# A gated product that reads its gate in PSUM, four output buffers, an undivided last row and a new order list

## The chip, the cores and the metric

The kernel runs on one core of one Trainium2 chip. The metric is the device time of one execution in microseconds; before the change the median of three runs was 163.64 us (162.80, 163.64, 165.22). A core has five engines that run side by side and wait for each other by semaphores: TensorE (PE, matrix products, results in PSUM), VectorE (DVE), ScalarE (ACT), GpSimd (POOL) and SyncE (SP, here only an issuer of DMAs).

## The reference

Sliding-window attention with sink tokens, and behind it a gated feed-forward block over the same sequence. Four batches, 8 heads of 64, 768 positions, window 128, 4 sinks; in the second half 512 model columns and 2 x 512 hidden columns.

```
scores = q @ k.T / 8, kept where key < 4 or 0 <= query - key < 128
x      = softmax(scores) @ v            # heads side by side: 4 x 768 x 512
h      = gelu(x @ w_in)                 # 1024 columns
u, v   = h[..., :512], h[..., 512:]
v_n    = (v - mean) / sqrt(var + 1e-6) * g_ln
v_s    = w_sg @ v_n + b_sg              # along the 768 positions
out    = x + (u * v_s) @ w_out
```

## The kernel before

The attention works on pairs of heads: 16 pairs n, four to a batch. For a pair, k and q are loaded, cast to bf16 on POOL or DVE (cast_k, cast_q), turned on PE and copied out of PSUM (turn, cols), or turned by a DMA for the last pairs. The scores come in three groups per pair (sc), an exponential on ACT leaves PSUM (exp), a mask is put on by DVE or POOL (band), the values are summed on PE (pv), and DVE divides (rcp, x). x is turned to columns xT by PE or by a DMA.

The block works on a batch b. hv makes the v half, 128 positions at a time, hu the u half, 128 hidden columns f by 384 positions (half m). ACT puts the gelu on (gelu_v, gelu_u), DVE takes mean and variance (bn), vn is the normalised v. The spatial product is eight tiles per batch: for f and m, six matmuls in two parts (sp..a, sp..b) fill half a bank of PSUM (tile vs); gate multiplies by g and adds the bias b_bc on DVE; gT multiplies by u into the tile gT, bf16 in SBUF. Then six projections pj of 128 positions each read gT, o adds x on DVE into an output buffer o_sb and a store issued on SP sends it out.

No engine chooses its order at run time. FIRST lists all operations by name, and `Planner.run` emits them in that order, so each engine's program is the sublist that falls on it. TAKERS says which engine takes an operation that several could do. A name has the batch or pair first: gate201 is batch 2, f = 0, m = 1; pj23 is batch 2, row 3. `Room` counts buffers: PSUM has six banks for these tiles, two in room s (scores, and in the last batch also vs and o_ps) and four in room m (everything else); o_sb has three buffers, gv two. In the last batch the output may also use the buffers of k_f and q_f.

Lines that the prediction speaks of: L858 the spatial matmul, L870 gate, L878 gT, L902 the projection, L913 o, L922 the store, L248 casts and copies on DVE or POOL, L632 and L630 the masks on DVE, L305 and L310 the masks on POOL, L670 the values, L689 x.

Of the kernel before, what the change touches and what calls it, by code (L numbers as in the profile page):

```python
# [49 lines left out]
class Planner:  # L50
# [40 lines left out]
    "load_k0 iden blank warm night dark nil zero_b0 zero_a0 zero_a2 zero_a3 load_q0 raw_a low_a "  # L91
# [86 lines left out]
def kernel(  # L178
# [65 lines left out]
    def copy(e, dst, src):  # L244
        if e == "ACT":
            nc.scalar.copy(dst, src)
        else:
            eng[e].tensor_copy(dst, src)  # L248


    NV = 6
    WARM = 8
    AHEAD = (0, 1)
    HALVES = 4
    LONG = ()
    BY_DMA = (11,12,13,14,15)
# [1068 lines left out]
```

## Time and profile before

| | us |
|---|---|
| median of three runs | 163.64 |
| the profiled execution | 162.83 |
| its span, first to last instruction | 161.1 |
| PE busy | 152.0 |
| DVE busy | 129.4 |
| ACT busy | 106.1 |
| POOL busy | 84.4 |
| first hv matmul of batches 0, 1, 2, 3 | 26.2, 66.75, 98.26, 129.69 |
| last matmul group ends | 155.85 |

The span is what the trace shows of the execution; the 1.7 us around it belong to the time too. In the rows that follow, a group of instructions is named by its line, engine and operation, with output and inputs; x8 is a count. A row of a stretch (from:to) gives its length, the busy time of each engine in it with the number of instructions, the granted clock, and the share of the DMA engines. A row of the timeline begins with start and duration in us.

### The profile page before, as it was taken

What the parts mean: (1) busy time and instruction counts of PE and PEld (TensorE: products, weight loads), DVE (VectorE), ACT (ScalarE), POOL (GpSimd) and SP (SyncE); (2) the same over time, 40 slices, a digit from 0 to 9 for tenths busy, and PEclk for the clock granted to TensorE, in tenths of its full rate; (3) what the DMA queues carried; (4) which work ended last, traced back from release to release, by engine and by line L of the source; (5) the groups of instructions that cost most, each with busy time, mean ns of one, the idle gap of its engine ahead of it and who ended that gap; (6) DMA issues with size and microseconds to landing.
All of it is one profiled execution on the core that took longest, in us unless ns stands there. A gap on an engine that the chain in (4) does not pass through costs nothing.

```text
span 161.1 us, 4019 instructions
## 1 busy us (share of the span) xinstructions
PE 152.0 (94%) x1562; PEld 88.1 (55%) x1562; DVE 129.4 (80%) x283; ACT 106.1 (66%) x142; POOL 84.4 (52%) x127
## 2 busy tenths in 40 slices
PE   6899999999999799999999999999999999999960
PEld 2346565576656656456656654455575645565530
DVE  3768486889799998497999889779998779768870
ACT  6368887789977687878967776684887158910100
POOL 3342891067859958777956745189568402300000
PEclk9999999999999999999999999999999999999998
DMA  4969999999999789899798799999922942030182
GB/s 152 352 171 312 204 179 191 226 348 336 327 233 307 222 103 260 210 347 284 180 215 195 192 186 276 194 259 214 215 81 78 162 157 78 2 135 1 69 319 78
DMA packets 67878, 32.43 MB, mean 201 GB/s; under 512 B 56564, under 2 KB 64772, under 8 KB 67856
## 3 DMA queue, kind: packets, MB, share of 16 engines
q1 hardware_dynamic: 65472, 29.39, 71.5%
q0 software_dynamic: 2384, 2.75, 10.7%
q8 instruction: 13, 0.21, 0.6%
q14 instruction: 9, 0.07, 0.1%
HBM read 24.81 MB, written 6.29 MB: 193 GB/s over the span
## 4 chain that ended last, share of the span: by engine, by line
PE 65%; DVE 19%; DMA 8%; issue 3%; ACT 1%; POOL 1%; SPq 0%; DVEq 0%; POOLq 0%
PE vs L858 14%; PE o_ps L902 10%; PE hv L745 10%; PE hu L787 10%; PE sc L604 7%; DMA out_dram<-o_sb 5%; PE av L670 5%; PE sc L584 4%; PE cps L544 3%; DVE o_sb L913 3%; DVE x L689 3%; DMA q_f<-in_q_dram 2%; DVE gv L870 2%; DVE st L767 2%; DVE ex L632 2%
## 5 line engine op out<-in xcount | busy, mean ns | idle before, releaser
L621 ACT ACTIVATE ex<-sc 128x1024 bf16<-128x1024 f32 x48 | 47.4, 1025 | 14.2 <-PE sc L604 14.2
L858 PE MATMUL vs<-wsgT,vn 128*128 128x384 bf16 x192 | 35.4, 327 | 0.1
L795 ACT ACTIVATE uT<-hu 128x384 bf16<-128x384 f32 x32 | 15.3, 490 | 14.3 <-PE hu L787 14.0
L858 PEld LDWEIGHTS <-vn 128*128 128x128 bf16 x192 | 17.6, 98 | 12.6 <-issue 1.3
L902 PE MATMUL o_ps<-w_out_sb,gT 128*128 128x512 bf16 (+1 forms) x100 | 23.7, 371 | 0.1
L787 PE MATMUL hu<-xT,w_in_sb 128*128 128x384 bf16 x128 | 23.1, 326 | 0.0
L305 POOL TENSOR_SCALAR_AFFINE_SELECT ex<-ex 128x512 bf16<-128x512 bf16 (+1 forms) x24 | 15.9, 663 | 13.5 <-ACT ex L621 13.3
L745 PE MATMUL hv<-w_in_sb,xT 128*128 128x512 bf16 x96 | 22.2, 379 | 0.3 <-DMA xT<-x 0.2
L870 DVE SCALAR_TENSOR_TENSOR gv<-vs,g_sb,b_bc 128x384 bf16<-128x384 f32 x32 | 19.3, 611 | 2.3 <-PE vs L858 1.7
L913 DVE TENSOR_TENSOR o_sb<-o_ps,x 128x512 f32<-128x512 f32 (+1 forms) x25 | 16.3, 663 | 4.5 <-PE o_ps L902 2.3
L767 DVE BATCH_NORM_STATS2 st<-v_all 128x6 f32<-128x512 f32 x24 | 16.2, 674 | 4.1 <-ACT v_all L756 4.0
L604 PE MATMUL sc<-qT,kT 64*128 64x256 bf16 (+2 forms) x320 | 19.0, 251 | 0.0
L670 PEld LDWEIGHTS <-ex 128*128 128x128 bf16 x480 | 16.2, 97 | 4.2 <-issue 2.1
L670 PE MATMUL av<-v_sb,ex 128*128 128x65 bf16 x352 | 17.3, 193 | 1.0 <-DVE o_sb L913 1.0
L689 DVE TENSOR_TENSOR x<-av,rcps 128x384 bf16<-128x384 f32 x32 | 17.3, 554 | 0.8
L878 DVE TENSOR_TENSOR gT<-gv,uT 128x384 bf16<-128x384 bf16 x32 | 15.8, 507 | 1.5 <-ACT uT L795 0.5
L787 PEld LDWEIGHTS <-w_in_sb 128*128 128x128 bf16 x128 | 12.3, 98 | 8.1
L756 ACT ACTIVATE v_all<-hv 128x512 f32<-128x512 f32 x24 | 13.5, 598 | 4.5 <-PE hv L745 4.2
L248 POOL CAST cast<-k_f 128x768 bf16<-128x768 f32 x14 | 12.5, 891 | 7.5 <-DMA k_f<-in_k_dram 7.4
L745 PEld LDWEIGHTS <-xT 128*128 128x128 bf16 x96 | 9.1, 98 | 11.5 <-DMA xT<-x 0.7
L248 POOL CAST v_sb<-v_f 128x768 bf16<-128x768 f32 x16 | 13.5, 860 | 3.1 <-DMA v_f<-in_v_dram 3.0
L248 POOL CAST cast<-q_f 128x768 bf16<-128x768 f32 x14 | 12.6, 898 | 4.6 <-DVE cast L248 2.3
(69 smaller groups left out, 198.8 us busy)
## 6 DMA issues: line engine op xcount, KB each, us to landing
k_f<-in_k_dram SPq DMA_DIRECT2D x16, 384.0 KB, 5.2
q_f<-in_q_dram SPq DMA_DIRECT2D x16, 384.0 KB, 5.2
v_f<-in_v_dram SPq DMA_DIRECT2D x16, 384.0 KB, 6.5
out_dram<-o_sb SPq DMA_DIRECT2D x23, 256.0 KB, 3.8
wsg<-in_moe_w_sg_dram POOLq DMA_DIRECT2D x2, 576.0 KB, 10.4
w_in_sb<-in_moe_w_in_dram POOLq DMA_DIRECT2D x2, 512.0 KB, 6.8
w_out_sb<-in_moe_w_out_dram POOLq DMA_DIRECT2D x1, 512.0 KB, 8.4
b_bc<-in_moe_b_sg_dram SPq DMA_DIRECT2D x1, 384.0 KB
```

Of the source, the lines that this page charges most:

```text
L248: eng[e].tensor_copy(dst, src)
L604: nc.tensor.matmul(sc.tile[row:row + keys, h, col:col + m], kT.tile[rows, k0:k0 + keys], qT.tile[rows, q0:q0 + m], start=not by_pe, stop=n ...
L621: nc.scalar.activation(out=ex.tile, in_=sc.tile, func=AF.Exp, scale=scale)
L670: nc.tensor.matmul(av.tile[:, m, h, :], ex.tile[:, h, col:col + 128], val, start=first, stop=(m == HT - 1 and h == 1 and at == len(steps) ...
L689: nc.vector.tensor_mul(x.tile[:, hp, HT * c:HT * (c + 1), :].rearrange("p i (h d) -> p i h d", h=2), av.tile[:, :, :, 0:64], rcp.to_broadc ...
L745: nc.tensor.matmul(ps.tile[:, 0:512], xT.tile[:, c, 128 * j:128 * (j + 1)], w_in_sb[:, c, DF:], start=(c == 0), stop=(c == KD - 1))
L767: nc.vector.bn_stats(out=st.tile, in_=v_all.tile[:, j, :])
L787: nc.tensor.matmul(ps.tile[:, 0:NH], w_in_sb[:, c, 128 * f:128 * (f + 1)], xT.tile[:, c, NH * m:NH * (m + 1)], start=(c == 0), stop=(c == ...
L858: nc.tensor.matmul(ps.tile[:, 0:NH], vn.tile[:, si, 128 * f:128 * (f + 1)], wsgT[:, si, cols], start=(si == 0), stop=(si == NT - 1))
L870: nc.vector.scalar_tensor_tensor(out=gv.tile, in0=ps.tile[:, 0:NH], scalar=g_sb[:, f:f + 1], in1=b_bc[:, cols], op0=ALU.mult, op1=ALU.add)
L902: nc.tensor.matmul(ps.tile[:, 0:w], gT.tile[:, c, 128 * t:128 * (t + 1)], w_out_sb[:, c, cols], start=(c == 0), stop=(c == KU - 1))
L913: nc.vector.tensor_add(o_sb.tile[:, 0:w].rearrange("p (h d) -> p h d", d=128), ps.tile[:, 0:w].rearrange("p (h d) -> p h d", d=128), x.til ...
```

## The change

Gate no longer writes a bf16 tile gv in SBUF: it writes its result back over the f32 tile vs in PSUM, and gT reads it there. So the bank is held until gT is done. The room gv goes down to one buffer, which only the general path uses, and o_sb has four buffers in place of three. The projection of the last batch's row 4 is no longer made in two column halves (HALVES). The planning costs of gT and of the stores are changed in the program's text, and FIRST and TAKERS are new as a whole; of them one line stands here.

```diff
-    "store11 gT211 pj21 cols_x15 store22 hv30 o21 store21 hv34 gT201 gelu_v30 hv32 gelu_v32 "
+    "xT12 store14 xT13 xT14 pj22 o22 store03 sp221a turn_x15 cols_x15 gate201 sp221b gate221 "
...
-        s=2, m=4, k_f=4, q_f=4, v_f=4, cast=4, cast_v=2, kT=5, qT=4, ex=8, x=2, xT=2,
-        v_all=1, mv=2, uT=2, vn=2, gT=2, gv=2, o_sb=3, st=4).items()}
+        v_all=1, mv=2, uT=2, vn=2, gT=2, gv=1, o_sb=4, st=4).items()}
...
-    HALVES = 4
+    HALVES = None
...
-        ps, gv = Buf([R[r] for r in rooms]), Buf(R["gv"])
+        ps = Buf([R[r] for r in rooms])
...
         def gate(_):
-            gv.tile = tile_of("gv")
             nc.vector.scalar_tensor_tensor(
-                out=gv.tile, in0=ps.tile[:, 0:NH], scalar=g_sb[:, f:f + 1], in1=b_bc[:, cols],
-                op0=ALU.mult, op1=ALU.add)
+                out=ps.tile[:, 0:NH], in0=ps.tile[:, 0:NH], scalar=g_sb[:, f:f + 1],
+                in1=b_bc[:, cols], op0=ALU.mult, op1=ALU.add)
...
-            nc.vector.tensor_mul(gT.tile[:, f, cols], gv.tile, uT.tile[:, f, cols])
+            nc.vector.tensor_mul(gT.tile[:, f, cols], ps.tile[:, 0:NH], uT.tile[:, f, cols])
...
-            f"gT{b}{f}{m}", {"DVE": 500 if b < B - 1 else 365}, mul,
+            f"gT{b}{f}{m}", {"DVE": 560}, mul,
...
-            use=[gv, uT, gT], rank=rank - 1)
+            use=[ps, uT, gT], rank=rank - 2000)
```

In TAKERS, the casts of k0, q0, q1 and k3 go from DVE to POOL and that of q2 the other way; the masks band72 and band81 go from POOL to DVE and band41 the other way; of the 24 vn, DVE has 16 in place of 17; the copy of k4 goes from ACT to DVE and that of k5 from DVE to ACT.

Three places show how the programs of the engines move. The first is DVE in the spatial stage of batch 0, from its first gate on; before, with gv as the gate's output:

```order
L870 SCALAR_TENSOR_TENSOR gv<-vs,g_sb,b_bc 128x384
L248 COPY kT<-cps 128x768
L870 SCALAR_TENSOR_TENSOR gv<-vs,g_sb,b_bc 128x384
L878 TENSOR_TENSOR gT<-gv,uT 128x384 x2
L632 TENSOR_TENSOR ex<-ex,mask_71 128x1024
L870 SCALAR_TENSOR_TENSOR gv<-vs,g_sb,b_bc 128x384
L630 TENSOR_TENSOR ex<-ex,mask 128x2x384
L870 SCALAR_TENSOR_TENSOR gv<-vs,g_sb,b_bc 128x384
L878 TENSOR_TENSOR gT<-gv,uT 128x384
```

And DVE at the same place now:

```order
L869 SCALAR_TENSOR_TENSOR vs<-vs,g_sb,b_bc 128x384
L877 TENSOR_TENSOR gT<-vs,uT 128x384
L869 SCALAR_TENSOR_TENSOR vs<-vs,g_sb,b_bc 128x384
L877 TENSOR_TENSOR gT<-vs,uT 128x384
L632 TENSOR_TENSOR ex<-ex,mask_71 128x1024
L869 SCALAR_TENSOR_TENSOR vs<-vs,g_sb,b_bc 128x384 x2
L877 TENSOR_TENSOR gT<-vs,uT 128x384 x2
L869 SCALAR_TENSOR_TENSOR vs<-vs,g_sb,b_bc 128x384
```

Each gT now follows its gate at once or behind one more gate; the copy of kT and the mask of 384 columns are gone from between them.

The second place is POOL at the head of the program, from the two masks of the constant tile on, where the first casts of k and q stand; before:

```order
L305 AFFINE_SELECT ex<-ex 128x2x128
L310 AFFINE_SELECT ex<-ex 128x2x128
L390 MEMSET vsink 4x8
L248 CAST vsink<-raw 4x8x64
L248 CAST cast<-k_f 128x2x6x64 x2
L248 CAST cast<-q_f 128x2x6x64
L248 CAST v_sb_74<-v_f 128x12x64
L248 CAST cast<-q_f 128x2x6x64
L248 CAST v_sb_75<-v_f 128x12x64
L427 DMA w_in_sb<-in_moe_w_in_dram 128x4x512
```

POOL at the same place now:

```order
L305 AFFINE_SELECT ex<-ex 128x2x128
L310 AFFINE_SELECT ex<-ex 128x2x128
L248 CAST cast<-k_f 128x2x6x64
L248 CAST cast<-q_f 128x2x6x64
L248 CAST cast<-k_f 128x2x6x64
L248 CAST cast<-q_f 128x2x6x64
L248 CAST cast<-k_f 128x2x6x64
L248 CAST v_sb_74<-v_f 128x12x64
L248 CAST cast<-k_f 128x2x6x64
L248 CAST cast<-q_f 128x2x6x64
```

The sink rows (vsink) have gone to DVE, and the first two pairs are cast on POOL; the load of w_in is issued next behind these rows, ahead of the second cast of v.

The third place is DVE at the end of its program, from the last spatial tiles to the last output; before:

```order
L870 SCALAR_TENSOR_TENSOR gv<-vs,g_sb,b_bc 128x384
L878 TENSOR_TENSOR gT<-gv,uT 128x384
L913 TENSOR_TENSOR o_sb<-o_ps,x 128x512 x3
L913 TENSOR_TENSOR o_sb<-o_ps,x 128x256
L913 TENSOR_TENSOR o_sb<-o_ps,x 128x512
L913 TENSOR_TENSOR o_sb<-o_ps,x 128x256
L913 TENSOR_TENSOR o_sb<-o_ps,x 128x512
```

DVE at the same place now:

```order
L912 TENSOR_TENSOR o_sb<-o_ps,x 128x512
L869 SCALAR_TENSOR_TENSOR vs<-vs,g_sb,b_bc 128x384
L877 TENSOR_TENSOR gT<-vs,uT 128x384 x2
L912 TENSOR_TENSOR o_sb<-o_ps,x 128x512 x6
```

Behind the last gT stand six outputs of full width in place of five and two halves. On PE both programs end with pj23, and on SP with store23.

More of the change, by code (lines that the diff above doesn't have):

```diff
@@ L90 @@
 FIRST = (
[L91 removed]
[64 rows of a table removed]
+    "load_k0 iden load_q0 raw_a night blank nil zero_a3 zero_a1 zero_b3 warm zero_a0 dark mask "
[64 rows of a table added]
 )
 TAKERS = (
[L158 to L161 removed]
@@ L162 @@
-    "cols_k2:DVE cast_q2:POOL cols_q2:DVE cols_x2:ACT cast_k3:DVE cols_k3:ACT cast_q3:POOL "
-    "cols_q3:DVE cols_x3:DVE vn00:DVE vn01:DVE vn02:DVE vn03:DVE vn04:DVE vn05:ACT cols_k4:ACT "
-    "cols_q4:ACT band41:DVE band42:POOL cols_k5:DVE cols_q5:ACT band51:POOL band52:POOL "
+    "zero_a0:ACT zero_a1:DVE zero_a2:DVE zero_a3:DVE low_a:DVE zero_b0:DVE zero_b1:DVE "
+    "zero_b2:ACT zero_b3:DVE low_b:POOL cols_g:DVE cols_w0:DVE cols_w1:ACT cols_w2:ACT "
+    "cols_w3:DVE cols_w4:DVE cols_w5:DVE cast_k0:POOL cols_k0:DVE cast_q0:POOL cols_q0:ACT "
@@ L165 @@
+    "cols_x0:ACT cast_k1:POOL cols_k1:DVE cast_q1:POOL cols_q1:DVE cols_x1:ACT cast_k2:POOL "
+    "cols_k2:DVE cast_q2:DVE cols_q2:DVE cols_x2:DVE cast_k3:POOL cols_k3:ACT cast_q3:POOL "
+    "cols_q3:DVE cols_x3:DVE vn00:DVE vn01:DVE vn02:ACT vn03:ACT vn04:DVE vn05:DVE cols_k4:DVE "
+    "cols_q4:ACT band41:POOL band42:POOL cols_k5:ACT cols_q5:ACT band51:POOL band52:POOL "
     "cols_k6:ACT cols_q6:ACT band61:POOL band62:POOL cols_k7:ACT cols_q7:ACT band71:POOL "
-    "band72:POOL cols_x7:DVE cols_k8:ACT cols_q8:ACT band81:POOL band82:POOL vn10:DVE vn11:DVE "
@@ L170 @@
+    "band121:POOL band122:POOL vn20:DVE vn21:DVE vn22:ACT vn23:ACT vn24:ACT vn25:DVE "
     "band131:POOL band132:POOL band141:POOL band142:POOL band151:POOL band152:POOL cols_x15:ACT "
-    "vn30:DVE vn31:DVE vn32:ACT vn33:ACT vn34:DVE vn35:ACT"
+    "vn30:DVE vn31:ACT vn32:ACT vn33:ACT vn34:DVE vn35:DVE"
 )
```

14 lines of the change are left out of this document (5 added, 9 removed), and 126 rows, old and new, of the table FIRST.

## The prediction

> **What bounds the kernel now.** I read the page first: busy time of each engine, then the chain that ended last.
>
> ```profile
> span 161.1 us, 4019 instructions
> PE 152.0 (94%) x1562; PEld 88.1 (55%) x1562; DVE 129.4 (80%) x283; ACT 106.1 (66%) x142; POOL 84.4 (52%) x127
> PE 65%; DVE 19%; DMA 8%; issue 3%; ACT 1%; POOL 1%; SPq 0%; DVEq 0%; POOLq 0%
> ```
>
> TensorE is busy 94% of the span and holds 65% of the chain; VectorE comes second with 80% and 19%. An average hides the stages, so next I cut the span at the first hv matmul of each batch, with one more cut where the spatial matmuls of batch 0 begin.
>
> ```profile
> core 0: us, PE busy (x) PEld busy (x) DVE busy (x) ACT busy (x) POOL busy (x), PEclk, DMA share, GB/s
> 26.00:40.46 14.46, 14.46 (x126) 8.86 (x126) 11.26 (x25) 12.47 (x22) 6.01 (x10) 1.00 1.12 286
> 40.46:66.75 26.29, 25.28 (x337) 16.02 (x337) 23.32 (x44) 20.34 (x24) 21.46 (x29) 1.00 1.00 246
> 66.75:98.26 31.51, 31.13 (x341) 17.98 (x340) 27.83 (x58) 25.39 (x34) 22.05 (x33) 1.00 0.97 221
> 98.26:129.69 31.43, 31.29 (x315) 17.98 (x315) 27.45 (x60) 19.82 (x28) 19.06 (x30) 1.00 0.90 185
> 129.69:155.85 26.16, 26.12 (x146) 14.05 (x144) 21.25 (x49) 10.41 (x18) 2.51 (x4) 1.00 0.25 94
> ```
>
> From 26.00 to 155.85 us PE is idle for 129.85 - 128.29 = 1.6 us (the sums of these rows), and the clock is full throughout. So little can be won in the middle: only the stretch from 40.46 has a PE gap of 1.01 us. In the third and fourth stretch DVE is busy 88% and 87% beside a full PE, with 3.7 and 4.0 us of room. The chain through the second stretch says who holds PE there, and the waits put a size on it.
>
> ```profile
> 53.53 1.00 DVE gT L878 x2
> 54.53 0.57 issue
> 55.11 0.69 DVE o_sb L913
> 55.79 0.04 issue
> 55.84 0.71 PE av L670 x18
> ...
> PE av L670 <- DVE o_sb L913: 1.0, 1, 1.0
> DVE o_sb L913 <- DMA out_dram<-o_sb: 2.1, 2, 1.4
> ```
>
> There gT and o run on DVE while PE waits for the bank that o frees: the 1.0 us. DVE itself waits 2.1 us in two places for an output buffer that a store still reads.
>
> **The multiplication gT.** It goes from two bf16 tiles in SBUF to one f32 operand in PSUM and one in SBUF. The rows of the same engine show both kinds (ns: least, median, most).
>
> ```profile
> L878 DVE TENSOR_TENSOR gT<-gv,uT x32: 344/359/1305, 43.6 to 151.4; 128x384 bf16<-128x384 bf16 x32
> L870 DVE SCALAR_TENSOR_TENSOR gv<-vs,g_sb,b_bc x32: 601/611/618, 41.6 to 150.3; 128x384 bf16<-128x384 f32 x32
> L689 DVE TENSOR_TENSOR x<-av,rcps x32: 518/557/559, 20.1 to 126.6; 128x384 bf16<-128x384 f32 x32
> L913 DVE TENSOR_TENSOR o_sb<-o_ps,x x25: 414/683/692, 55.1 to 155.9; 128x512 f32<-128x512 f32 x23, 128x256 f32<-128x256 f32 x2
> ```
>
> The nearest row to the new gT is x: 128x384, one operand in PSUM, 557 ns. I take 557, against a median of 359 now. But today's gT spreads up to 1305 ns, and the three kinds with one operand in PSUM hardly spread at all (601 to 618). What stretches it stands beside it on POOL:
>
> ```profile
> 53.26 0.82 POOL L248 CAST v_sb<-v_f 128x768 bf16<-128x768 f32 x1
> 54.02 0.95 POOL L248 CAST cast<-k_f 128x768 bf16<-128x768 f32 x1
> ...
> 53.45 1.74 DVE L878 TENSOR_TENSOR gT<-gv,uT 128x384 bf16<-128x384 bf16 x2
> ```
>
> Two gT take 1.74 us while POOL casts without a pause. So the price must be taken batch by batch (gT alone):
>
> ```profile
> core 0: us, DVE busy (x), PEclk, DMA share, GB/s
> 41.00:56.00 15.00, 5.79 (x8) 1.00 1.04 275
> 80.00:101.00 21.00, 3.62 (x8) 1.00 0.99 213
> 111.00:135.00 24.00, 3.66 (x8) 1.00 0.65 146
> 135.00:154.00 19.00, 2.78 (x8) 1.00 0.16 59
> ```
>
> Afterwards each batch has 8 x 0.557 = 4.46 us of gT: **-1.3 us in batch 0, +0.8 in batches 1 and 2 each, +1.7 in batch 3**, together +2.0 us of DVE.
>
> The Trainium skill, "VectorE: DVE Perf Modes", section "The perf-mode tier table", speaks against the change: a tensor_tensor of bf16 in SBUF runs at two results a cycle, with any PSUM operand at one. By that alone every gT would cost 557 - 344 = 0.21 us more, 6.8 us over 32; the trace agrees on the bare durations (344 against 557) and not on the sum, since the batches above already pay for the stretching.
>
> **The sum, stage by stage.**
>
> - Batch 0 (40.46 to 66.75). gT gives 1.3 us back; the kT copy of pair 4 (a DVE COPY of 0.95 us here) now stands ahead of the first gate; one more full mask product (row below) is on DVE. That is -1.33 - 0.95 + 0.73 = -1.55 us of DVE. PE idled 1.01 us. What is late next is ACT, whose exponentials feed the values, busy 20.34 of 26.29. I take **-0.7 us**, ends -1.5 and 0.
>
> ```profile
> L632 DVE TENSOR_TENSOR ex<-ex,mask x12: 675/730/1304, 45.1 to 122.1; 128x1024 bf16<-128x1024 bf16 x12
> 42.12 0.95 DVE L248 COPY kT<-cps 128x768 bf16<-128x768 bf16 x1
> ```
>
> - Batches 1 and 2. +1.6 us of DVE beside a PE with 0.5 us of gaps. DVE's room in those stretches (3.7 and 4.0 us) covers it on average, but gates come in bunches and PE waits for the banks they free; half of it shows: **+0.8**, ends 0 and 1.6.
> - Batch 3. +1.7 on DVE, 21.25 + 1.7 = 22.95 us against 26.16 of PE: hidden, **0**. The last gT ran from 151.43 and its first reader comes after two projections that don't need it (5.35 / 6 = 0.89 us each), so 0.2 us more is covered too.
>
> ```profile
> 149.81 0.81 PE L787 MATMUL hu<-xT,w_in_sb 128*128 128x384 bf16 x4
> 150.46 5.35 PE L902 MATMUL o_ps<-w_out_sb,gT 128*128 128x512 bf16 x28
> ...
> 151.43 0.36 DVE L878 TENSOR_TENSOR gT<-gv,uT 128x384 bf16<-128x384 bf16 x1 [0.47 <-ACT uT L795]
> 155.85 0.69 DVE L913 TENSOR_TENSOR o_sb<-o_ps,x 128x512 f32<-128x512 f32 x1 [0.20 <-PE o_ps L902]
> ```
>
> - The bank. Until now gate freed it; now gT does, 0.6 us later, and where gT has to wait for u, later still. Queued behind a waiting gT are the other gates, rcp and x of the attention, and PE waits for their banks. Batches 0 to 2 share four banks, so 24 x 0.6 / 4 = 3.6 us is the upper end; lower end 0, since the new order issues gT right behind its gate. Near the lower end, because PE has almost no gaps on banks now: **+0.5**.
> - The gate's write. No row shows DVE writing PSUM. Its f32 output is wider; o, with f32 output, takes 683 ns for 512 elements and x, with bf16, 557 for 384, which is 0.98 ns for each of 128 more elements: width costs nothing. I take 0. Ends: 0.07 us each way (gate against o, 683 - 611), 2.3 us over 32, both ways since a write to another memory may end sooner or later.
> - Output buffers. The 2.1 us of waits may go; one was in front of the statistics of batch 1, but store03 now stands behind o22, so o03 keeps its buffer through batches 1 and 2 and three are left to turn. **-0.3**, ends -2.1 and 0.
> - The head. The casts of k0 and q0 go from DVE to POOL. q0 is on the chain:
>
> ```profile
> 5.40 0.82 DVE cast L248
> ...
> L248 POOL CAST cast<-q_f 128x768 bf16<-128x768 f32 x14 | 12.6, 898 | 4.6 <-DVE cast L248 2.3
> 18.19 0.98 POOL L427 DMA_DIRECT2D w_in_sb<-in_moe_w_in_dram  x1
> ```
>
> 898 - 820 is +0.08, and POOL does four casts in a row where DVE took part: **+0.2**, upper end one cast, 0.9. POOL also issues the w_in load (18.19); it is behind one cast of v fewer and three casts of k and q more, of which POOL waited 2.3 us for one, so it moves little.
> - The last row undivided: one o of 0.68 for two of 0.42, PE's 28 matmuls in the tail become 24 of the same columns, and both programs end with pj23, o23 and its store: 0.
> - The rest of the new order (stores, loads, casts, hu and sp exchanged within their batch) leaves the work of each engine as it was; on SP's queue stores 10, 11, 14 and 00 come earlier, 03, 05, 15 and 20 later, each an issue on a queue with nothing busy behind it but loads. I price it at 0, ends -1 and +1.
>
> Sum: -0.7 + 0.8 + 0 + 0.5 + 0 - 0.3 + 0.2 = **+0.5 us** on the profiled execution of 162.83 us, so 163.3. The median of the three runs is 163.64, 0.8 above that execution; on the median's scale I say **164.1 us**.
>
> **Rivals.**
>
> 1. *The stretching goes and carries more with it: 162.4.* If gT no longer meets POOL, POOL's own casts get shorter too (1.28 us for the one at 48.73, against 0.82 at 53.26), so batch 0 gains its whole 1.5 us, DVE's waits for buffers go with 1.0, and batches 1 and 2 stay hidden under PE: 163.64 - 1.5 - 1.0 + 0.8 + 0.5 = 162.4. For it: the spread of gT and its absence with one PSUM operand. Against: PE has only 1.6 us of gaps. The Trainium skill has this as a rule ("SBUF — State Buffer", section "Who interferes with whom"): two SBUF inputs on DVE contend with a reading POOL, one does not; the trace agrees as far as the rows go (601 to 618 against 344 to 1305).
>
> ```profile
> 48.73 1.28 POOL L248 CAST cast<-k_f 128x768 bf16<-128x768 f32 x1
> ```
>
> 2. *Banks become the bound: 167.2, slower.* In the spatial stages of batches 0 to 2 PE finds all four banks held by results waiting for gT. It decides once the extra hold, 0.6 us for each of 24, is no longer covered by banks that stand empty; in full it is 3.6 us: 163.64 + 3.6 = 167.2. Against it: in the order, hardly a gate has more than one operation before its gT.
> 3. *Writing PSUM is dear: 166.1.* +0.07 us on each gate as well; 2.3 us on a DVE that has 3.7 us of room in a stretch, of which most shows in batches 0 to 2: 164.1 + 2.0.
> 4. *The buffers do not turn:* o03 parks one and nothing is gained there, while the rest holds: 164.4, inside the forecast's own case.
>
> **How the numbers follow.** The forecast with rival 4 has 0.54, rival 1 0.23, rival 2 0.12, rival 3 0.11. Two per cent of 163.64 is 3.3 us, about what a measurement of this kernel can tell from no change: faster below 160.4, slower above 166.9. Rival 1 passes the lower bound only with both unknown costs at their good ends (0.05 in all); rival 2 passes the upper one, and rival 3 in part: 0.13. Within: 0.82. The range reaches from 161.8, a little past rival 1, to 166.6, past rival 3; rival 2 stays outside.
>
> **What would show it.** gT with a median near 557 ns and a most below 600; the gate at 611; eight gT of batch 0 in 4.5 us; the PE gap near 55 us gone or shorter; gate and gT back to back on DVE. I am wrong if PE rows L858 or L670 wait for DVE gT for more than 1 us in sum, if the gate is over 0.68, or if hv of batch 1 starts over 1 us later than 66.75.

## The result, and the profile after

The changed kernel takes 162.5 us, the median of 20 runs (161.09 to 166.14), beside 163.72 us for the kernel before in 20 runs on the same chip (162.73 to 165.27). The ratio is **0.9912, with a 95% interval of 0.9883 to 0.9941**: a little faster, where the forecast was a little slower. The time lies in the predicted range and within 2% of the time before, but +0.5 us was forecast and -1.2 us came. (Ratios, here and below, leave out executions that took over 1.5% longer than the fastest of the same kernel, medians keep them, so the two do not agree in every row; the profiled executions of b_zero and a_gv2 are of that kind.)

The profiled execution took 161.09 us, with a span of 159.2 us against 161.1. First the page of the changed kernel: its span, the busy times of the engines, and the shares of the chain that ended last.

```profile
span 159.2 us, 4002 instructions
PE 150.8 (95%) x1558; PEld 87.1 (55%) x1558; DVE 130.0 (82%) x281; ACT 107.5 (68%) x143; POOL 83.5 (52%) x126
PE 76%; DVE 7%; DMA 7%; POOL 3%; ACT 2%; SPq 1%; issue 1%; POOLq 0%; ACTq 0%
```

DVE has gone from 19% of the chain to 7%, and PE from 65% to 76%. The busy times hardly moved. Next the view by stretches of the changed kernel, cut at the first hv matmul of each batch and at the end of the last projection. The table behind it has the kernel before cut at the same places (its first hv matmuls start at 26.08, 66.75, 98.26 and 129.53).

```profile
core 0: us, PE busy (x) PEld busy (x) DVE busy (x) ACT busy (x) POOL busy (x), PEclk, DMA share, GB/s
24.58:65.06 40.48, 39.75 (x461) 24.99 (x459) 34.65 (x73) 33.41 (x45) 26.84 (x38) 1.00 1.01 249
65.06:96.40 31.34, 30.64 (x342) 18.10 (x341) 28.03 (x58) 25.37 (x34) 20.88 (x30) 1.00 0.96 215
96.40:127.24 30.84, 30.84 (x311) 17.27 (x310) 27.26 (x59) 20.72 (x29) 19.67 (x31) 1.00 0.94 210
127.24:154.40 27.16, 27.14 (x147) 14.15 (x145) 22.88 (x47) 10.62 (x18) 2.51 (x4) 1.00 0.24 90
```

| stretch | before | after | difference |
|---|---|---|---|
| start to the first hv matmul of batch 0 | 26.08 | 24.58 | -1.50 |
| to the first hv of batch 1 | 40.67 | 40.48 | -0.19 |
| to the first hv of batch 2 | 31.51 | 31.34 | -0.17 |
| to the first hv of batch 3 | 31.27 | 30.84 | -0.43 |
| to the end of the last projection | 26.28 | 27.16 | +0.88 |
| to the end | 5.3 | 4.8 | -0.5 |

The four stretches from the first hv to the end of the last projection, which hold all of gate and gT, come to 129.7 us before and 129.8 after. The +0.88 of batch 3 is one thing: pj20 stood ahead of hv30 and stands behind hv35 now, and a projection is 0.89 us of PE. With it left out, batch 2 is 0.45 us longer and not 0.43 shorter. What is left is the head, -1.50, and the tail, -0.5. The tail is the same work in another execution: two repeats of the changed kernel (after2 and after3, below) had 5.3 and 5.0 there.

Now the groups of the two operations that the change rewrites (ns: least, median, most), and gT alone in the spatial stage of each batch.

```profile
L877 DVE TENSOR_TENSOR gT<-vs,uT x32: 542/557/558, 41.7 to 149.8; 128x384 bf16<-128x384 f32 x32
...
L869 DVE SCALAR_TENSOR_TENSOR vs<-vs,g_sb,b_bc x32: 609/616/626, 41.0 to 148.6; 128x384 f32<-128x384 f32 x32
```

```profile
core 0: us, DVE busy (x), PEclk, DMA share, GB/s
38.00:56.00 18.00, 4.34 (x8) 1.00 1.20 300
78.00:101.00 23.00, 4.36 (x8) 1.00 0.97 197
108.00:135.00 27.00, 4.44 (x8) 1.00 0.61 152
135.00:154.00 19.00, 4.31 (x8) 1.00 0.25 97
```

gT now costs 557 ns wherever it stands, and the spread up to 1305 ns is gone. The gate costs 616 ns for 611. These are the predicted sizes, almost to the digit, and they are not where the time went.

### The profile page after: what moved, and what is told of

The parts are those of the page before. It is cut to its first block, busy times and chain, and to the rows that moved or that the text cites. A ratio compares the mean times of both kernels' runs of the same rounds, so it can differ in the third digit from the quotient of the medians.

```text
span 159.2 us, 4002 instructions
## 1 busy us (share of the span) xinstructions
PE 150.8 (95%) x1558; PEld 87.1 (55%) x1558; DVE 130.0 (82%) x281; ACT 107.5 (68%) x143; POOL 83.5 (52%) x126
## 3 DMA queue, kind: packets, MB, share of 16 engines
HBM read 24.81 MB, written 6.29 MB: 195 GB/s over the span
## 4 chain that ended last, share of the span: by engine, by line
PE 76%; DVE 7%; DMA 7%; POOL 3%; ACT 2%; SPq 1%; issue 1%; POOLq 0%; ACTq 0%
PE vs L858 20%; PE o_ps L901 12%; PE hv L745 10%; PE sc L604 9%; PE av L670 8%; PE hu L787 7%; PE cps L544 4%; PE sc L584 3%; DMA k_f<-in_k_dram 3%; DMA q_f<-in_q_dram 2%; DVE vn L834 2%; PE xps L720 2%; POOL cast L248 2%; DMA xT<-x 1%; DVE o_sb L912 1%; DVE mv L820 1%
## 5 line engine op out<-in xcount | busy, mean ns | idle before, releaser
L901 PE MATMUL o_ps<-w_out_sb,gT 128*128 128x512 bf16 x96 | 23.0, 379 | 0.0
L869 DVE SCALAR_TENSOR_TENSOR vs<-vs,g_sb,b_bc 128x384 f32<-128x384 f32 x32 | 19.5, 619 | 2.6 <-PE vs L858 1.3
L305 POOL TENSOR_SCALAR_AFFINE_SELECT ex<-ex 128x512 bf16<-128x512 bf16 (+1 forms) x23 | 15.4, 670 | 9.4 <-ACT ex L621 9.1
L248 POOL CAST cast<-k_f 128x768 bf16<-128x768 f32 x16 | 13.4, 836 | 12.1 <-DMA k_f<-in_k_dram 12.0
L670 PEld LDWEIGHTS <-ex 128*128 128x128 bf16 x480 | 16.7, 97 | 4.1 <-issue 1.4
L877 DVE TENSOR_TENSOR gT<-vs,uT 128x384 bf16<-128x384 f32 x32 | 17.4, 554 | 0.9
L670 PE MATMUL av<-v_sb,ex 128*128 128x65 bf16 x352 | 18.0, 194 | 0.1
L912 DVE TENSOR_TENSOR o_sb<-o_ps,x 128x512 f32<-128x512 f32 x24 | 16.2, 684 | 1.5 <-PE o_ps L901 1.4
```

Of the source, the lines that this page charges most:

```text
L670: nc.tensor.matmul(av.tile[:, m, h, :], ex.tile[:, h, col:col + 128], val, start=first, stop=(m == HT - 1 and h == 1 and at == len(steps) ...
L869: nc.vector.scalar_tensor_tensor(out=ps.tile[:, 0:NH], in0=ps.tile[:, 0:NH], scalar=g_sb[:, f:f + 1], in1=b_bc[:, cols], op0=ALU.mult, op1 ...
L877: nc.vector.tensor_mul(gT.tile[:, f, cols], ps.tile[:, 0:NH], uT.tile[:, f, cols])
L901: nc.tensor.matmul(ps.tile[:, 0:w], gT.tile[:, c, 128 * t:128 * (t + 1)], w_out_sb[:, c, cols], start=(c == 0), stop=(c == KU - 1))
L912: nc.vector.tensor_add(o_sb.tile[:, 0:w].rearrange("p (h d) -> p h d", d=128), ps.tile[:, 0:w].rearrange("p (h d) -> p h d", d=128), x.til ...
```

## The experiments

In this table the first-hv column is of the profiled execution, and "from there" is the time from the first hv to the end of the last projection (before: 26.08 and 129.7; after: 24.58 and 129.8). Each kernel ran beside the kernel before on the same chip; the runs are spread over several chips. All compute the whole result.

| kernel | ratio to before | 95% interval | first hv | from there |
|---|---|---|---|---|
| b_gate: before, gate in PSUM | 1.0635 | 1.0515 to 1.0754 | 26.62 | 137.8 |
| b_gate_mv: the same, gT right behind its gate | 1.0016 | 0.9977 to 1.0056 | 25.04 | 129.8 |
| b_head: before, new order up to the first hv | 1.0006 | 0.9953 to 1.0059 | 24.80 | 130.8 |
| b_head2: repeat | 0.9888 | 0.9832 to 0.9944 | 25.02 | 132.0 |
| b_both: b_gate_mv with the new head | 0.9986 | 0.9946 to 1.0026 | 25.23 | 131.2 |
| a_gv: after, gate and gT through SBUF | 1.0117 | 0.9966 to 1.0269 | 24.68 | 131.9 |
| a_gv2: repeat | 1.0051 | 1.0013 to 1.0088 | - | - |
| a_head: after, old order up to the first hv | 0.9993 | 0.9927 to 1.0060 | 26.43 | 129.1 |
| b_o4: before, four output buffers | 1.0079 | 1.0035 to 1.0122 | 26.48 | 130.6 |
| a_halves: after, last row in halves | 0.9963 | 0.9920 to 1.0006 | 24.70 | 129.7 |
| a_rstd: after, rstd03 earlier | 0.9948 | 0.9906 to 0.9990 | 25.03 | 130.3 |
| after2: the changed kernel again | 0.9860 | 0.9779 to 0.9940 | 24.91 | 130.1 |
| after3: the changed kernel again | 0.9908 | 0.9875 to 0.9941 | 24.92 | 129.6 |
| b_zero: before, one name moved | 0.9922 | 0.9890 to 0.9955 | - | - |
| b_zero2: repeat | 0.9905 | 0.9866 to 0.9944 | 24.90 | 129.9 |
| a_zero: after, that name late | 0.9945 | 0.9904 to 0.9986 | 25.07 | 131.0 |
| b_headz: b_head, that name late | 0.9962 | 0.9922 to 1.0003 | 25.69 | 131.3 |
| a_sp: after, loads ahead of the vsink copies | 0.9973 | 0.9939 to 1.0007 | 26.62 | 130.7 |

### The two parts apart: gate in PSUM, and the head

b_gate takes the kernel before with its old order, and changes gate and gT alone.

```diff
-        ps, gv = Buf([R[r] for r in rooms]), Buf(R["gv"])
+        ps = Buf([R[r] for r in rooms])
...
-                out=gv.tile, in0=ps.tile[:, 0:NH], scalar=g_sb[:, f:f + 1], in1=b_bc[:, cols],
+                out=ps.tile[:, 0:NH], in0=ps.tile[:, 0:NH], scalar=g_sb[:, f:f + 1],
...
-            nc.vector.tensor_mul(gT.tile[:, f, cols], gv.tile, uT.tile[:, f, cols])
+            nc.vector.tensor_mul(gT.tile[:, f, cols], ps.tile[:, 0:NH], uT.tile[:, f, cols])
```

> The kernel before with one edit: gate writes back to PSUM and gT reads it there; order list, three output buffers and the divided row as before. Theory R (the relief of gT from POOL is the gain): a ratio near 0.993, eight gT of batch 0 in 4.5 us instead of 5.8, and the hv of batch 1 about 1 us earlier than 66.75. Theory H (the gain of 1.2 us comes from the head of the new order): 1.000 within 0.003, since with the old order gT often stands far behind its gate and the bank is held (up to 64 places in the list). Theory B (banks, my rival 2): above 1.005 with this order, PE waiting for gT.

It is 6% slower. Its stretches of batches 1 and 2 and, out of batch 2, rows of PE with a wait and rows of DVE:

```profile
68.35:101.71 33.36, 31.43 (x340) 18.09 (x340) 28.16 (x58) 25.16 (x34) 21.61 (x33) 1.00 1.01 226
101.71:137.57 35.86, 31.98 (x311) 17.97 (x314) 29.45 (x61) 20.12 (x28) 19.29 (x29) 1.00 0.68 154
```

```profile
129.71 0.66 PE L858 MATMUL vs<-wsgT,vn 128*128 128x384 bf16 x3 [0.89 <-DVE x L689]
...
133.30 1.04 PE L901 MATMUL o_ps<-w_out_sb,gT 128*128 128x512 bf16 x3 [0.88 <-DVE x L689]
...
135.12 0.65 PE L858 MATMUL vs<-wsgT,vn 128*128 128x384 bf16 x3 [0.78 <-DVE o_sb L912]
```

```profile
121.98 0.62 DVE L869 SCALAR_TENSOR_TENSOR vs<-vs,g_sb,b_bc 128x384 f32<-128x384 f32 x1
...
134.98 0.55 DVE L877 TENSOR_TENSOR gT<-vs,uT 128x384 bf16<-128x384 f32 x1
```

In the stretch of batch 2 PE stands idle for 35.86 - 31.98 = 3.9 us, waiting for banks that x and o free. In the old order two gT of this batch stand far behind their gates: in SBUF the gate's result waited there at no cost, in PSUM it keeps a bank. Between gate231 at 121.98 and gT231 at 134.98 lie 13 us. This is rival 2, banks as the bound, in a stronger form than it was priced: 8 us more from the first hv to the end of the last projection (137.8 against 129.7).

b_gate_mv differs from b_gate only in the order list: each gT is moved up to stand right behind its gate, or behind the gelu of its u where that is later.

```diff
-    "band130 gate231 sc141 exp141 pv120 pv121 sc142 store13 band131 pv130 band140 rcp121 x121 "
...
-    "band152 gate211 pv140 rcp140 pv141 rcp141 x141 x140 sp221a xT14 pv150 rcp150 x150 sp221b "
-    "pv151 rcp151 x151 pj22 o22 sp201a gT231 compare gate221 gT221 turn_x15 sp201b gate201 "
-    "store11 gT211 pj21 cols_x15 store22 hv30 o21 store21 hv34 gT201 gelu_v30 hv32 gelu_v32 "
...
+    "sp231b exp140 band130 gate231 gT231 sc141 exp141 pv120 pv121 sc142 store13 band131 "
...
+    "sp211a xT13 sc152 exp152 sp211b band152 gate211 gT211 pv140 rcp140 pv141 rcp141 x141 "
...
```

> The kernel before with gate in PSUM, as in the run with 1.06, but each gT stands right behind its gate (one of them 7, one 3 places behind, where u comes late); all else, the three output buffers too, in the old order. Theory: the 8 us of that run are banks held by a gT that stands far behind, and without that the relief from POOL shows even in the old order: 0.990 to 0.996. Rival: the old order has no room for the hold of 0.6 us at all, the new order was needed throughout: above 1.005.

1.0016, between the two outcomes that were expected, and 129.8 us from the first hv on, as before. So holding the result in PSUM costs and brings nothing, provided that gT follows its gate: the whole 6% was the place of gT in the order.

b_head goes the other way: gate and gT stay in SBUF, and all that stands ahead of hv00a in the order list, with the engines given to it, is taken from the change.

```diff
-    "load_k0 iden blank warm night dark nil zero_b0 zero_a0 zero_a2 zero_a3 load_q0 raw_a low_a "
-    "mask load_k1 cast_k0 cast_q0 load_q1 load_k2 load_q2 dark0 mask0 zero_a1 vsink_a1 vsink_a2 "
+    "load_k0 iden load_q0 raw_a night blank nil zero_a3 zero_a1 zero_b3 warm zero_a0 dark "
+    "mask ones cast_k0 cast_q0 dark0 zero_a2 load_k1 turn_k0 low_a load_q1 load_k2 load_q2 "
...
-    "cols_w3:DVE cols_w4:DVE cols_w5:DVE cast_k0:DVE cols_k0:ACT cast_q0:DVE cols_q0:ACT "
+    "cols_w3:DVE cols_w4:DVE cols_w5:DVE cast_k0:POOL cols_k0:DVE cast_q0:POOL cols_q0:ACT "
...
```

> The kernel before, but everything ahead of the first hv matmul in the order of the changed kernel and by its engines (sink rows on DVE, the first casts of k and q on POOL, the wide mask and the second part's zeros behind); the rest as before. Theory H: a ratio near 0.991, first hv at 24.8 us instead of 26.2, and the 1.4 us kept to the end. Theory R: 1.000 within 0.003; the head's gain is lost again by the stretch behind it, as 0.8 of 1.5 us was in the changed kernel by the start of the spatial stage.

> The kernel before with the new head alone, again, because median (0.991) and the ratio of the runs (1.001) of the first time disagree. If the head's 1.4 us reach the end in the old order: 0.990 to 0.994. If they are given back in batch 0, as its trace says (39.8 for the first spatial matmul, 66.25 for the hv of batch 1): 0.996 to 1.000.

The two results differ, 1.0006 and 0.9888, and their intervals do not meet: not settled by timing. In the trace the first hv came at 24.80 and 25.02, nearly as early as in the changed kernel, but both profiled executions lose that again by the end of the last projection (130.8 and 132.0 against 129.7). b_both, with both parts in the old order of the middle, loses 1.5 us there (131.2) and has 0.9986 in all:

> The kernel before with two parts of the change: gate in PSUM with gT right behind it, and the new head; three output buffers, divided row and the old order for the rest. If these two parts are the change: 0.989 to 0.994, as the changed kernel beside it. If the order of the middle is needed: 0.996 or more, with the spatial stage of batch 0 taking 26.0 us and not 25.3.

The opposite cut is a_gv: the changed kernel with its new order, and gate and gT through SBUF again (gv=2; a few small constants share tiles, so that the two buffers fit).

```diff
-        ps = Buf([R[r] for r in rooms])
+        ps, gv = Buf([R[r] for r in rooms]), Buf(R["gv"])
...
-            nc.vector.tensor_mul(gT.tile[:, f, cols], ps.tile[:, 0:NH], uT.tile[:, f, cols])
+            nc.vector.tensor_mul(gT.tile[:, f, cols], gv.tile, uT.tile[:, f, cols])
```

> The changed kernel with gate and gT through SBUF again (two gv buffers; some small constants share tiles so that these fit); order, engines and four output buffers as changed. Theory R: the gain goes, ratio to the kernel before 0.998 to 1.003, gT spread out to over 1 us again in batch 0. Theory H: 0.990 to 0.994, the same as the changed kernel.

> The changed kernel with gate and gT through SBUF, again, because the first interval was 0.997 to 1.027. If the gate in PSUM is worth over 1 us in the new order: at least 0.006 above the changed kernel beside it. If the first run's 2 us were scatter: within 0.004 of it.

On one chip a_gv2 took 165.43 us and the changed kernel (after2) 163.06: by these medians undoing this part alone costs 1.4% (2.4 us), and the intervals of the two ratios do not meet. The price per operation explains none of it. First gT of a_gv by its group, then its gT in batch 0 alone, then its stretch of batch 1 and a row of PE there:

```profile
L878 DVE TENSOR_TENSOR gT<-gv,uT x32: 345/358/1547, 42.2 to 152.0; 128x384 bf16<-128x384 bf16 x32
```

```profile
38.00:56.00 18.00, 5.74 (x8) 1.00 1.15 287
```

```profile
65.89:98.11 32.22, 30.52 (x340) 18.07 (x340) 27.73 (x58) 25.41 (x34) 20.70 (x30) 1.00 1.08 212
```

```profile
80.87 0.66 PE L858 MATMUL vs<-wsgT,vn 128*128 128x384 bf16 x3 [1.59 <-DVE vn L834]
```

The same place in the changed kernel:

```profile
79.15 0.66 PE L858 MATMUL vs<-wsgT,vn 128*128 128x384 bf16 x3 [0.70 <-DVE vn L834]
```

gT is 358 ns again, stretches up to 1547, and takes 5.74 us in batch 0 (4.34 in PSUM): the two prices and the stretching come back as the prediction read them. In batch 1, where gT is cheaper in SBUF, the stretch is longer (32.22 against 31.34 us), with a wait of 1.59 us for vn at a place where the changed kernel waits 0.70 (1.02 and 0.95 in after2 and after3). So the new order is slower with the SBUF form; which instruction is first late there was not followed up.

### The head

a_head is the changed kernel with the old order and engines up to hv00a (the diff of b_head, reversed).

> The changed kernel with the old order and engines ahead of the first hv matmul. Theory H: ratio to the kernel before 0.998 to 1.002, first hv at 26.2 us. Theory R: 0.990 to 0.994.

0.9993: with the old head the gain is gone, and the first hv is at 26.43, while the rest is as short as ever (129.1 us from there). The middle of the changed kernel is as long as that of the kernel before, so the net gain is in the head; a_gv shows that the new order needs the gate in PSUM to keep it. What in it? First the view by time of SP's queue (start, duration) in the kernel before, and SP's wait in its first 14 us (total, times, longest):

```profile
3.83 0.47 SPq L449 DMA_DIRECT2D q_f<-in_q_dram  x1
7.55 2.03 SPq L400 DMA_DIRECT2D vsink<-vsink  x3
9.63 0.45 SPq L459 DMA_DIRECT2D v_f<-in_v_dram  x1
10.12 0.69 SPq L449 DMA_DIRECT2D k_f<-in_k_dram  x1
```

```profile
SPq L400 <- DVE vsink L373: 3.2, 1, 3.2
```

The same two views of the changed kernel:

```profile
6.24 1.98 SPq L400 DMA_DIRECT2D vsink<-vsink  x3
8.26 0.45 SPq L459 DMA_DIRECT2D v_f<-in_v_dram  x1
8.75 0.69 SPq L449 DMA_DIRECT2D k_f<-in_k_dram  x1
```

```profile
SPq L400 <- DVE vsink L248: 1.9, 1, 1.9
```

SP issues in order. From 4.30 (3.83 + 0.47) on it holds the small vsink copies, which wait for zero_a1, a memset of 0.28 us on DVE that the old order puts behind two casts and the masks. Behind the copies stand the loads of v0, k3 and q3. The new order has zero_a1 among DVE's first instructions, and SP moves on 1.3 us sooner. So that single name was moved, in the kernel before:

```diff
-    "load_k0 iden blank warm night dark nil zero_b0 zero_a0 zero_a2 zero_a3 load_q0 raw_a low_a "
-    "mask load_k1 cast_k0 cast_q0 load_q1 load_k2 load_q2 dark0 mask0 zero_a1 vsink_a1 vsink_a2 "
+    "load_k0 iden blank warm night dark nil zero_b0 zero_a0 zero_a2 zero_a3 zero_a1 load_q0 "
+    "raw_a low_a mask load_k1 cast_k0 cast_q0 load_q1 load_k2 load_q2 dark0 mask0 vsink_a1 "
```

> The kernel before with one name moved in the order list: zero_a1, a memset of 0.28 us on DVE, from behind the masks to the front. Theory S (SP's queue): SP issues the sink rows at 5.9 us instead of 7.55, the loads of v0 and k3 come 1.6 us earlier, the first hv at 24.8 instead of 26.1, and a ratio of 0.989 to 0.994, like the new head as a whole. Theory C (the casts): first hv near 26, ratio 0.998 to 1.002.

> The kernel before with zero_a1 moved to the front, again, for a trace. Theory S: SP issues the sink rows at 5.9 to 6.8 us instead of 7.55, first hv 0.8 to 1.4 us before 26.1, ratio 0.989 to 0.995.

0.9922 and 0.9905, both clear of 1: **moving one memset alone gives as much as the whole change.** SP in b_zero2, and its wait, now for POOL:

```profile
5.79 2.03 SPq L404 DMA_DIRECT2D vsink<-vsink  x3
7.87 0.45 SPq L463 DMA_DIRECT2D v_f<-in_v_dram  x1
```

```profile
SPq L404 <- POOL vsink L252: 1.4, 1, 1.4
```

Two kernels put zero_a1 late within the new head: a_zero is the changed kernel, b_headz is b_head.

```diff
-    "load_k0 iden load_q0 raw_a night blank nil zero_a3 zero_a1 zero_b3 warm zero_a0 dark mask "
+    "load_k0 iden load_q0 raw_a night blank nil zero_a3 zero_b3 warm zero_a0 dark mask ones "
...
-    "cols_k0 cast_k1 turn_q0 cols_q0 dark00 cast_q1 cast_k2 sc00 dark01 exp00 turn_k1 cols_k1 "
+    "cols_k0 zero_a1 cast_k1 turn_q0 cols_q0 dark00 cast_q1 cast_k2 sc00 dark01 exp00 "
```

> The changed kernel with zero_a1 alone moved back, behind DVE's first copy of k; low row and casts as changed. Theory S: SP issues the sink rows at 7.3 instead of 6.2, the first hv comes 0.8 to 1.1 us later, and the ratio rises to 0.994 to 1.000. Theory C: as the changed kernel beside it within 0.003.

> The kernel before with the new head, but zero_a1 late, behind DVE's first copy of k, so that SP issues the sink rows at 7.3 us as before. If zero_a1 is the head's only gain: 0.998 to 1.002. If the casts on POOL and the sink row on DVE have one of their own: 0.990 to 0.996 and the first hv at 25.0 to 25.4.

> The changed kernel again, as the measure for the three beside it on the same chip: 0.989 to 0.994.

> The changed kernel again, as the measure for the three beside it on the same chip: 0.986 to 0.994.

The changed kernel again has 0.9860 and 0.9908. a_zero has 0.9945 beside 0.9908 of the changed kernel on the same chip, and b_headz 0.9962 beside 0.9905 of b_zero2: both are higher, and both intervals overlap with that of the other kernel. By time alone, what zero_a1 is worth inside the new head is not separated from nothing.

The trace, though, does not show PE waiting for the late loads in the kernel before. Here is PE in its head, and then in the changed kernel:

```profile
6.26 0.82 PE L544 MATMUL cps<-iden,cast 128*128 128x128 bf16 x6 [0.70 <-DVE cast L248]
6.88 1.06 PE L584 MATMUL sc<-ex,iden 128*128 128x512 bf16 x2
7.97 0.61 PE L604 MATMUL sc<-qT,kT 64*128 64x256 bf16 x4
...
9.91 0.52 PE L604 MATMUL sc<-qT,kT 64*32 64x128 bf16 x12
```

```profile
5.93 0.51 PE L544 MATMUL cps<-iden,cast 128*128 128x128 bf16 x6
6.27 0.59 PE L584 MATMUL sc<-ex,iden 128*128 128x512 bf16 x2
7.32 0.39 PE L604 MATMUL sc<-qT,kT 64*128 64x256 bf16 x4 [0.46 <-ACT qT L246]
...
8.41 0.52 PE L604 MATMUL sc<-qT,kT 64*32 64x128 bf16 x12
```

The transposes of q0 start 0.33 us later before, and the same matmuls take 0.82 for 0.51, 1.06 for 0.59 and 0.61 for 0.39 us, up to 9.91. There the kernel before is 1.50 us behind, and that is exactly what it is behind at the first hv: from there on both heads run PE without a gap to speak of. So **in this pair of executions the difference is a slow PE (1.17 us) and a q0 that landed 0.4 us later (0.33), not the late loads**, which the slow PE covers. q0's load is issued at 1.40 and 1.41 us, so zero_a1 has no part in the second, and no run ties it to the first. PE was slow until its full clock was granted, at 9.86 us before and at 5.75 after (last section).

One execution of each kernel is thin evidence, but there are twenty with the same work in the head. The table gives the start of q0's transposes and, in the last column, how much longer than 18.65 us (the changed kernel's own time) it took from there to the first hv.

| kernel | zero_a1 | q0 turns at | first hv | over 18.65 | seen there |
|---|---|---|---|---|---|
| before | late | 6.26 | 26.08 | 1.17 | PE slow |
| b_o4 | late | 6.35 | 26.48 | 1.48 | PE slow |
| a_head | late | 6.38 | 26.43 | 1.40 | PE slow from 7.23 |
| b_gate | late | 6.06 | 26.62 | 1.91 | waits for casts |
| b_gate_mv | late | 5.69 | 25.04 | 0.70 | a wait for a cast |
| b_headz | late | 6.29 | 25.69 | 0.75 | waits for casts |
| a_zero | late | 5.88 | 25.07 | 0.54 | a wait for a cast |
| b_zero2, after, after2, a_rstd | early | 5.93 to 6.37 | 24.58 to 25.03 | 0.00 to 0.01 | |
| a_gv, a_halves, b_head | early | 5.94 to 6.05 | 24.68 to 24.80 | 0.06 to 0.10 | |
| after3, b_both | early | 5.95, 6.25 | 24.92, 25.23 | 0.32, 0.33 | q0's transposes slow |
| b_head2 | early | 5.97 | 25.02 | 0.40 | a longer wait on POOL |
| a_sp | early | 6.81 | 26.62 | 1.16 | PE slow |
| b_zero | early | 7.20 | 28.04 | 2.19 | PE slow |
| a_gv2 | early | 6.18 | 25.77 | 0.94 | waits for casts |

With zero_a1 late it is 0.5 to 1.9 us more in seven of seven; with zero_a1 early 0 to 0.4 in ten of thirteen. That shows less than it seems to. Five of the long ones have a slow PE, one of them b_zero itself, the kernel before with nothing but zero_a1 early. And the cast that b_gate_mv and a_zero wait for, at 8.26 and 8.36 us, is that of k1, whose load stands ahead of the copies. Only in b_gate is it seen clearly that the late loads themselves hold PE up, with PE at its full rate:

```profile
14.55 0.41 PE L670 MATMUL av<-v_sb,ex 128*128 128x65 bf16 x8 [0.50 <-POOL v_sb L248]
...
18.36 0.51 PE L544 MATMUL cps<-iden,cast 128*128 128x128 bf16 x6 [0.66 <-POOL cast L248]
```

Those are the casts of v0 and q3, whose loads stand behind the vsink copies on SP (at 8.31 in that execution): 1.16 us. So the early memset can remove a wait of this kind where PE runs at full rate; that it also keeps PE from its slow rate is not shown. A rival stands untested: PE was slow in four of the seven executions with the old engines in the head (before, b_o4, a_head, b_zero) and in one of the thirteen with the new ones (a_sp), and the new head, which casts k0 and q0 on POOL, mostly leaves PE a shorter idle time ahead of q0's transposes. No run moves those casts alone. It does not explain b_zero's ratio, where they stay on DVE.

a_sp asks whether SP's queue can be shortened further: v0, k3 and q3 are issued ahead of the vsink copies, in the code as shown and in the order list alike.

```diff
+    load_rows("v", v, 0)
+    load_pair(3)
     for i in range(1, 4):
         set_out(i)
-    load_rows("v", v, 0)
-    load_pair(3)
```

> The changed kernel with the loads of v0, k3 and q3 issued by SP ahead of the three copies of the sink rows, for which SP waits until 6.2 us. Theory S: v0 and k3 land 2 to 4 us earlier; the first hv 0 to 0.8 us earlier, since PE and ACT are nearly full between 12 and 24 us: ratio 0.983 to 0.991. Theory C: no change against the changed kernel.

Nothing is gained: 0.9973, beside 0.9908 for the changed kernel and 0.983 to 0.991 expected. In the profiled execution SP issues the three loads from 4.33 us on, q0 is cast at 5.93 in place of 5.04 us, and PE is slow until 10.43.

### The smaller parts

b_o4 gives the kernel before a fourth output buffer (small constants share tiles to make room).

```diff
-        v_all=1, mv=2, uT=2, vn=2, gT=2, gv=2, o_sb=3, st=4).items()}
+        v_all=1, mv=2, uT=2, vn=2, gT=2, gv=2, o_sb=4, st=4).items()}
```

> The kernel before with four output buffers and nothing else (small constants share tiles so that they fit). If the buffers are part of the gain: the two waits of DVE for stores (2.1 us) gone and a ratio of 0.993 to 0.997. If not: waits gone or not, 1.000 within 0.003.

DVE's wait for stores in b_o4:

```profile
DVE o_sb L913 <- DMA out_dram<-o_sb: 0.9, 1, 0.9
```

The wait falls from 2.1 to 0.9 us, and the kernel is 0.8% slower (1.0035 to 1.0122), not faster. In the changed kernel the wait is not in the list at all. So the buffers do turn, and that is worth nothing here; neither expected outcome allowed for a slower kernel, and why b_o4 is slower was not found (its profiled head has PE slow, which is one execution).

a_halves cuts the changed kernel's last row in halves again; in the order list the two halves stand in the place of the whole.

```diff
-    HALVES = None
+    HALVES = 4
```

> The changed kernel with row 4 of the last batch in two halves again, at the place where the undivided one stood. As I priced it: nothing, the ratio of the changed kernel (0.991) within 0.003. If the undivided row is where the 0.4 us behind the last projection came from: 0.994.

0.9963 (0.9920 to 1.0006), where the changed kernel on another chip had 0.9912 (0.9883 to 0.9941): the ratio is above what was expected and the two intervals overlap, so whether the undivided row is worth 0 or some tenths of a per cent stays open. From the first hv to the end of the last projection the two take 129.7 and 129.8 us.

a_rstd came from the chain of the changed kernel, where the lead of 1.50 us at the first hv has shrunk to 0.63 at the first spatial matmul (39.77 against 40.40):

```profile
29.78 4.67 DMA k_f<-in_k_dram
...
34.58 0.86 POOL cast L248
...
35.52 0.83 POOL cast L248
...
36.75 0.90 POOL mv L814
```

k4 lands at 34.46, POOL casts k4 and q4, and only then does rstd03 come, which the spatial stage needs. In a_rstd it stands ahead of those casts, and the transposes of k4 and q4 stand later.

```diff
-    "hu021 gelu_u021 load_k4 load_q4 load_v4 cast_k4 cast_q4 mask0 cols_w4 turn_k4 cols_k4 "
-    "turn_q4 cols_q4 rstd03 shift03 vn03 vn05 hu030 turn_w5 turn_w3 gelu_u030 vn04 cols_w3 "
+    "load_v4 rstd03 cast_k4 cast_q4 mask0 cols_w4 shift03 vn03 vn05 hu030 turn_w5 turn_w3 "
+    "gelu_u030 turn_k4 cols_k4 turn_q4 cols_q4 vn04 cols_w3 cols_w5 sc40 sc41 exp40 b_bc "
```

> The changed kernel with one more move: the second root of the variance of batch 0 (rstd03, POOL) ahead of the casts of k4 and q4, whose loads POOL waited for, and the turns of k4 and q4 on PE behind the turns of w_sg that follow. Theory: the 0.8 of 1.5 us that the head's gain loses by 39.8 us is POOL's order; the first spatial matmul at 38.9 or earlier instead of 39.8 and a ratio of 0.986 to 0.989. Rival: PE has no other work to bring forward, the stretch behind is bound by the loads; the ratio of the changed kernel, 0.991, or worse.

The first spatial matmul came at 40.80, later and not earlier (0.45 us of that is a later first hv), because PE now waits for the copy of q4 that the scores of pair 4 read:

```profile
39.82 0.74 PE L608 MATMUL sc<-qT,kT 64*128 64x256 bf16 x16 [0.89 <-ACT qT L250]
```

The one wait was exchanged for the other; 0.9948 is no gain on 0.9912. Both hang on k4's load, and that load stands in SP's queue behind sink copies once more, those for the pairs of the later batches. These copies are issued at 27.77 us in the changed kernel and at 24.49 before, and k4's load at 29.78 and 27.40: 2.4 us later, though the first hv is 1.5 us earlier. The new order has put what the copies need (zero_b0, low_b) behind hv00a, and no run here moves it back. No kernel here is clearly faster than the changed one, and b_zero, one name away from the kernel before, is as fast.

## Why the prediction was right or wrong

- **What bounds the kernel: right.** PE has hardly a gap from the head to the end in both, and 129.7 against 129.8 us from the first hv to the end of the last projection says that the middle could neither win nor lose much.
- **The price of gT and gate: right.** 557 ns was taken for gT, 557 is the median; 4.46 us for a batch, 4.31 to 4.44 came. The gate was costed at 0 with ends of 0.07 us; it is +5 ns. The rule of the Trainium skill that the prediction cites, "VectorE: DVE Perf Modes", section "The perf-mode tier table", puts bf16 in SBUF at two results a cycle and any PSUM operand at one; the bare durations go that way, by a factor of 1.6 (358 ns in a_gv, 557 here). The stretching of bf16 in SBUF was real, since it came back in a_gv.
- **Batch 0, -0.7: right in its own stretch, and given back ahead of it.** DVE's share went as reckoned (gT -1.45 us), the PE gap of 1.0 us near 55 us is gone, and the stretch from the first spatial matmul to hv of batch 1 is 25.29 us against 26.35. But from the first hv to the first spatial matmul it is 15.19 against 14.32, 0.64 of it a PE that stands idle, which the terms left out; a wait of 0.57 there hangs on k4's load. From the first hv the whole is -0.19. (The kT copy of 0.95 us that the term takes from DVE is pair 5's, which goes to ACT, and not pair 4's; the sum is the same.)
- **Batches 1 and 2, +0.8, and the bank, +0.5: too much.** With the exchange of pj20 left out they became 0.17 us shorter and 0.45 longer, +0.3 in all. Most of DVE's added 1.5 us (4.36 + 4.44 for 3.62 + 3.66) stayed hidden. The bank term named its condition rightly: near the lower end, *since the new order issues gT right behind its gate*. b_gate shows that without it the upper end of 3.6 us was too low: 8 us.
- **Batch 3 and the last row, 0: right for gT.** The +0.88 there is pj20, not gT; the undivided row was not settled by a_halves.
- **Output buffers, -0.3: wrong.** DVE's waits for stores went, even with o03 parked, and b_o4 shows no gain from that.
- **The head, +0.2, with the rest of the new order at 0: this is the step that failed.** It put prices on the casts that change engines and on POOL's issue of w_in, and let the rest of the order stand at 0 with ends of 1 us, with SP as "a queue with nothing busy behind it but loads". SP's wait of 3.2 us for a memset, with loads behind it, was in the trace of before, and the new order takes 1.3 us of it away; moving that memset alone measures 0.9922 and 0.9905. Measured at the first hv: -1.50 in the profiled pair, and over the profiled executions a mean of 24.87 us (nine with the new head whole; 24.96 with a_gv2) against 26.13 (five with the old head whole), -1.3 us, which is the size of the measured gain. The casts on POOL, which the term did price, don't show: q0's transposes start at 5.69 to 6.38 with the casts on DVE (before, b_o4, a_head, b_gate, b_gate_mv, b_zero2) and at 5.88 to 6.37 with them on POOL, two odd cases apart (b_zero, 7.20, and a_sp, 6.81).
- **Rival 1 named nearly the time that came, 162.4 us, and not the reason.** It wanted the gain in batch 0 and in the buffers' waits; both waits went, and the time they gave was given back at k4's load. **Rival 2** is real and was kept away by the order. **Rival 3** falls with the gate's 616 ns.
- **The range held by luck.** The middle, where the terms were, came to 0 and the change of time came from the head, by more than the ends of its terms allowed. The signs named for gT and gate all came; they speak of the middle, and none of them looks at the head.

What stays open: by which path zero_a1 acts in most executions, and how much of the changed kernel's shorter head is due to it and how much to a PE that gets its full clock sooner. The trace shows SP freed 1.3 to 1.8 us earlier, and once (b_gate) PE waiting for what stood behind; in the profiled execution of the kernel before, a slow PE hides the same lateness.

## What to carry to other kernels

In a change that rewrites an order list, follow every in-order queue to the instruction that it stands on, however small: a memset of 0.28 us held a queue for 3.2 us with the loads of v0, k3 and q3 behind it, and moving it was worth as much as the whole change. Moving an intermediate from SBUF to PSUM costs by how long the bank is held, not by the operation: the same edit was 6% slower with the consumer far behind and even with the consumer next in line. And where two traces differ in the first microseconds, compare the durations of the same matmuls before looking for a wait.

## What the runs showed of the hardware

In these executions PE starts at half its rate, and the views do not say so. The trace keeps the granted clock as a list of entries with a start, a length and a share, and a view counts a stretch that no entry covers as 1.00. In the kernel before the list begins with the full clock at 9.86 us. So the 1.00 of the first row below is no reading; the second row lies behind 9.86 us, and its matmuls have the usual rate. Behind them stands the same place of a_head:

```profile
6.26:9.91 3.65, 3.61 (x21) 1.00 0.78 287
9.91:12.42 2.51, 2.51 (x31) 1.00 0.77 181
```

```profile
5.90:10.00 4.10, 3.28 (x28) 0.68 0.87 320
```

In a_head the list has the full clock from 3.99 us, half of it from 7.40 and the full clock again from 10.82, which is why its row reads 0.68. Both rows have the doubled matmuls (two of 512 columns in 1.06 and 0.87 us against 0.59). Ahead of them k0's six transposes show the same, here in the kernel before and then in a_head:

```profile
4.71 0.85 PE L544 MATMUL cps<-iden,cast 128*128 128x128 bf16 x6
```

```profile
4.71 0.51 PE L548 MATMUL cps<-iden,cast 128*128 128x128 bf16 x6 [0.18 <-DVE cast L252]
```

The first entry stands at 9.86 us in before, at 10.77 in b_o4, 10.43 in a_sp and 13.30 in b_zero, and at 3.99 to 6.94 in the other sixteen. It is not set by the kernel alone: b_zero2 is the same program as b_zero and has it at 6.07, and the changed kernel had it at 5.75, 6.26 and 6.70. The full clock that PE then keeps to the end of its work lasts 146.77 to 160.43 us; these lengths differ by multiples of 3.41 us, and a_head's two short entries last 3.41 us each. Ahead of q0's transposes PE stood idle for 0.70 to 1.64 us in the five executions with a late or a withdrawn full clock, and for 0.88 us at most in the others.

The Trainium skill, "TensorE: Matmul & The Clock Gate", section "Part 1: The HAM clock gate (the "warmup" mystery)", describes a gate that halves PE's clock by default and opens after a busy window of some 3.4 us, with a window that runs freely of the kernel's start. The steps of 3.41 us agree with that. That the idle time ahead of q0's transposes decides whether the window counts as busy is argued from these rows, and no run isolated it.
